# Queries and keys laid out by head pairs on GpSimd and transposed in 128x128 tiles

## The chip, the cores and the metric

The kernel runs on one core of one Trainium2 chip. The metric is device time in microseconds (us) for one execution. PE is TensorE, with PEld its weight loads, DVE is VectorE, ACT is ScalarE, POOL is GpSimd, SP is SyncE, which issues most DMAs. Each engine runs its own instructions in the order in which the program wrote them, and waits at semaphores for the others.

## The reference

Two layers follow each other: attention over chunks of 32 tokens with 8 memory slots per head, and a mixture of 8 experts with one expert a token.

```python
B, H, S, D = 4, 8, 768, 64                       # _attn_setup
for c in range(nc):                              # chunks of 32, 16 tokens left, 8 right
    k_full = np.concatenate([mem_k, k_ctx], axis=2)
    v_full = np.concatenate([mem_v, v_ctx], axis=2)
    scores = scale * np.matmul(q_c, k_full.transpose(0, 1, 3, 2))
    scores = scores - np.max(scores, axis=-1, keepdims=True)
    a = np.exp(scores)
    a = a / (np.sum(a, axis=-1, keepdims=True) + 1e-09)
    out[:, :, c_start:c_end] = np.matmul(a, v_full)
...
x = attn_out.transpose(0, 2, 1, 3).reshape(B * S, H * D)
logits = x @ w_gate                              # 8 experts, width 512 -> 1024 -> 512
disp[e, pos] = x[i]                              # in order of tokens, up to the capacity
h = np.maximum(np.einsum('ecd,edf->ecf', disp, w1), 0.0)
y = np.einsum('ecf,efd->ecd', h, w2)
out[i] = gate_w[i] * y[expert_idx[i], pos[i]]
```

## The kernel before

The attention stage works on 12 segments of 256 tokens (`segs`, 3 for each of 4 batches) and, within them, on 24 tiles of 128 tokens. One pass of `for t in range(NTL)` (L192) is one tile; even t begins segment t / 2. A segment's q and k come with one DMA each (`load_q`, `load_k`, 512 KB) into a ring of four slots in `raw2`: a partition holds two neighbouring tokens of one head side by side (`j` = 0, 1) and the 8 heads behind each other. They are loaded two segments ahead.

For the scores the head dimension has to stand on the partitions, with two heads (`hf` = 0, 1: an even and an odd head, a pair) on partitions 0 to 63 and 64 to 127. So q and k of segment n = t // 2 + 1 are transposed on PE one or two tiles ahead: `trans_k(n)` at even t, `trans_q(n)` at odd t, right behind the scores of the tile.

- `trans_q` (L453) makes 16 matmuls with the identity as the moving operand, each for one head and one `j`, 64 columns wide, into 64 partitions of a PSUM tile. The trace shows each as two passes. ACT copies two tiles of 128x512 into `qT` and interleaves the two tokens (L465).
- `trans_k` (L468) makes 8 transposes of 128x128 (L475), one for each head. The head's two tokens land on partitions 0 to 63 and 64 to 127, so ACT needs 8 copies of 64x256 (L480) into `KW`, one for each pair of `hf` and `j` and half of the heads. `KW` holds for each chunk of 32 tokens 24 keys of the chunks to the left, its own 32, and 8 memory keys. Then `copy_k` (L484) fills the 24: DVE does the odd heads, POOL the even ones from n = 2 on (L496, L498).

The rest of a tile: scores (L509, 16 matmuls), maximum and difference on DVE (L517, L520), exponent on ACT (L526), transposes of the weights of tile t - 1 (`trans_p`, L533), weights times values of tile t - 2 (`value`, L550) with the division on DVE (L553 to L558) and a column copy on POOL (L542), the transposes of the output (`trans_out`, L603) and the logits of earlier tiles. `VW` holds the values in two slots; `copy_v` (L414, L415) copies the overlaps on DVE, in part on ACT, and `load_v` brings the next 256 tokens in 8 DMAs. `route` decides each group's expert rows on DVE, and `put` (L803) writes rows of x to their slots with a DMA that POOL issues. From t = 14 to 21 POOL also subtracts for the split of the first expert's weights (L829), after ACT's cast (L828).

What sets the order is the program text alone: the block runs under `manual_schedule`, and each engine's queue is the order of the calls. POOL's queue is the one that the change touches most. Before the loop it fills `KW[1]` and `VW[1]` with zeros (L174, L136, L139) and the memory keys (L450); at t = 1 it makes the constants of the routing (L576 to L594); at t = 3 it copies the values of all memory slots (`memv`) into `ME` (L203), once their loads have landed. SP issues the loads of `memv` for the next batch at t = 0, 1 and 2 (L124), among those of k, q and v.

PSUM tiles come from a pool of 7 (`psum`). After the attention the experts run: `early` on the first 256 rows while routing ends, then `expert` for each of the 8.

Of the kernel before, what the change touches and what calls it, by code (L numbers as in the profile page):

```python
# [7 lines left out]
F32 = mybir.dt.float32  # L8
# [9 lines left out]
P = 128  # L18
B, H, S, DH, NMEM = 4, 8, 768, 64, 8
LEFT, CHUNK = 16, 32  # L20
# [30 lines left out]
class Kernel:  # L51
# [42 lines left out]
    def attention(self):  # L94
        tc, nc = self.tc, self.nc
# [5 lines left out]
        st = self.st  # L101
# [6 lines left out]
        memv = st.tile([64, 4, DH], F32, name="memv")  # L108
        self.ME = ME = st.tile([64, 2, 4, 65], F32, name="ME")
        self.preT = st.tile([P, 2, 8, B * H // 2], F32, name="preT")  # L110
        self.segs = segs = [(b, s) for b in range(B) for s in range(NSEG)]
        NS = len(segs)
        self.qn, self.kn, self.qT, self.pT, self.ex, self.xs = {}, {}, {}, {}, {}, {}
# [8 lines left out]
        def load_memv(b):  # L122
            for par in range(2):
                nc.sync.dma_start(out=memv[par * 32 + b * 8:par * 32 + b * 8 + 8],  # L124
                                  in_=self.mem_v[b].rearrange("(r u) m d -> u m r d", u=2)[par])
# [45 lines left out]
        for par in range(2):  # L171
            r = slice(par * 32, par * 32 + 8)
            nc.gpsimd.tensor_copy(out=ME[r, par, :, 0:64], in_=memv[r])
        nc.gpsimd.memset(KW[1][64:P, :, :, 0, :].rearrange("p a c d -> p (a c) d"), 0.0)  # L174
        self.fill_mem_v(0)
        self.load_k(2)
        self.load_q(2)
        zero_v(1, 0, None)
# [8 lines left out]
        def split1(t):  # L187
            if any(i == t for i, _ in PLAN):
                j = todo.pop(0)
                self.split(self.raw1, self.w1hi, self.w1lo, (slice(None), slice(None), slice(j, j + SPLIT1)), nc.gpsimd)  # L190

        for t in range(NTL):  # L192
            n = t // 2 + 1
            if t % 2 == 0 and n < NS:
                self.fill_mem_k(n)
            if t == 1:
                self.routing_setup()
            if t < 3:
                load_memv(t + 1)
            if t == 3:  # L200
                for par in range(2):
                    r = slice(par * 32, par * 32 + 32)
                    nc.gpsimd.tensor_copy(out=ME[r, par, :, 0:64], in_=memv[r])  # L203
            if t == 11:
                nc.sync.dma_start(out=self.raw1, in_=self.w1[0].rearrange("(k p) f -> p k f", p=P))
            self.scores(t)
            if n < NS:
                if t % 2 == 0:
                    self.trans_k(n)
                    if n + 2 < NS:  # L210
                        self.load_k(n + 2)
                else:
                    self.trans_q(n)
                    if n + 2 < NS:
                        self.load_q(n + 2)
            self.exps(t)
            if 0 <= t - 1 < NTL:
                self.trans_p(t - 1)
            if 0 <= t - 2 < NTL:
                self.value(t - 2)  # L220
            if 0 < t <= NTL - VB:
                self.copy_v(t - 1)
            k = (t - 2) // VB + 2
            if t > 1 and (t - 2) % VB == VB - 1 and k < B * NVB:
                self.fill_mem_v(k)
                self.load_v(k)
            if t == 22:

                nc.sync.dma_start(out=self.raw2, in_=self.w2[0].rearrange("(k p) d -> p k d", p=P))
            split1(t)  # L230
            self.tick(t > 20)
            if 0 <= t - 3 < NTL:
                self.trans_out(t - 3)
            if 0 <= t - 4 < NTL:
                self.logits(t - 4)
            for _ in range(3 if t > 20 else 1):
                self.tick(True)
            for _ in range(2 if t > 20 else 1):
                if self.puts:
                    self.put(*self.puts.pop(0)[:2])  # L240
            if t - 4 in ends:
                self.routes.append([self.route(ends[t - 4]), 1])
# [210 lines left out]
    def trans_q(self, n):  # L453
        nc = self.nc
        t = self.qT[n] = self.wk.tile([P, 4, SEG], F32, name="qT")
        src = self.qn.pop(n)
        for i in range(2):
            ps = self.psum().rearrange("p (r j t) -> p r j t", r=2, j=2)

            for r in range(2):  # L460
                for j in range(2):
                    for hf in range(2):
                        nc.tensor.matmul(ps[hf * 64:hf * 64 + 64, r, j, :], src[:, 4 * i + 2 * r + hf, j * 64:j * 64 + 64],  # L463
                                         self.ident, start=True, stop=True)
            (nc.vector.tensor_copy if n == 0 and i else nc.scalar.copy)(  # L465
                out=t[:, 2 * i:2 * i + 2, :].rearrange("p r (t j) -> p r j t", j=2), in_=ps)

    def trans_k(self, n):  # L468
        nc = self.nc
        kw = self.KW[n % NKW]  # L470
        src = self.kn.pop(n)
        for i in range(2):
            ps = self.psum().rearrange("p (h t) -> p h t", h=4)
            for h in range(4):
                nc.tensor.transpose(out=ps[:, h, :], in_=src[:, 4 * i + h, :], identity=self.ident)  # L475
            ps = ps.rearrange("p h (m t) -> p h m t", t=16)
            for hf in range(2):
                r = slice(hf * 64, hf * 64 + 64)
                for j in range(2):
                    (nc.vector.tensor_copy if n == 0 and i else nc.scalar.copy)(out=kw[r, 2 * i:2 * i + 2, :, hf, 24 + j:56:2], in_=ps[j * 64:j * 64 + 64, hf::2])  # L480
        if n:
            self.copy_k(n)

# [533 lines left out]
```

## Time and profile before

| what | value |
|---|---|
| median of 3 runs | 511.56 us |
| the three runs | 510.7, 511.56, 1536.18 us |
| the profiled execution | 508.52 us |
| its span, first to last instruction | 506.7 us |
| mean granted TensorE clock | 0.977 |
| PE, PEld busy | 461.3 us (91%), 394.1 us (78%) |
| DVE, ACT, POOL busy | 295.4 us (58%), 233.8 us (46%), 115.4 us (23%) |

One of the three runs took three times as long as the others; the median leaves it out. The two others and the profiled execution lie within 3.1 us. The page's strip by 40 slices of 12.7 us shows two stages: in the first 11 or 12 slices DVE and ACT are about as busy as PE, after that PE alone is near full. A row of the timeline gives start and length in us, engine, line, operation and operands, and in brackets for how long the engine had been idle and what ended that. Several equal instructions in a row are merged (x8).

### The profile page before, as it was taken

To read this page: it belongs to the slowest core of one execution; us is meant where nothing else is said; L and a number is where in the kernel's file an instruction comes from. 1 tells how busy PE (TensorE), PEld (TensorE's weight loads), DVE (VectorE), ACT (ScalarE), POOL (GpSimd) and SP (SyncE) were. 2 spreads that over 40 slices of the span, in tenths; PEclk is the share of its full clock that TensorE was granted. 3 is DMA by queue.
4 is the path that set the end of the run, shared out by engine and by line. 5 is a ranking of instruction groups with operands and counts; after the bars stand their busy time and mean duration, and the time that the engine had idled before them with its cause. 6 is when DMAs were issued, how large, how long until landed. Compare 5 with 4: busy or idle time off the path is not lost.

```text
span 506.7 us, 11689 instructions
## 1 busy us (share of the span) xinstructions
PE 461.3 (91%) x4317; PEld 394.1 (78%) x4317; DVE 295.4 (58%) x678; ACT 233.8 (46%) x462; POOL 115.4 (23%) x151
## 2 busy tenths in 40 slices
PE   7889988998868599898999999999999999889993
PEld 6778776777558579787888899799988989767782
DVE  6899797999854723456555525726442565554410
ACT  6799778888432413325434314524330553433300
POOL 8531133554623370020100210010022011020011
PEclk9999999999997899999999999999999999989997
DMA  9697899974672585227472480543321644630010
GB/s 212 152 213 157 198 272 261 208 200 104 134 273 93 177 303 169 108 70 266 160 243 61 156 294 15 190 154 125 125 87 50 217 172 167 225 115 2 4 41 38
DMA packets 77816, 78.71 MB, mean 155 GB/s; under 512 B 31762, under 2 KB 58510, under 8 KB 77648
## 3 DMA queue, kind: packets, MB, share of 16 engines
q1 hardware_dynamic: 72848, 61.93, 42.6%
q0 software_dynamic: 4800, 14.95, 7.7%
q8 instruction: 55, 0.90, 0.8%
q14 instruction: 113, 0.93, 0.6%
HBM read 60.86 MB, written 15.99 MB: 152 GB/s over the span
## 4 chain that ended last, share of the span: by engine, by line
issue 37%; DMA 34%; PE 16%; DVE 7%; ACT 2%; SPq 2%; POOLq 1%; DVEq 0%; POOL 0%; ACTq 0%
DMA out_dram<-y,tok 27%; DMA x_d<-pad,pads 4%; PE ps L509 3%; PE ps L463 3%; PE ps L550 3%; PE ps L533 2%; ACT kw L480 2%; DVE vw L415 1%; PE ps L332 1%; PE ps L475 1%; PE ps L603 1%; DMA raw<-in_q_dram 1%; DMA vw<-in_v_dram 1%; SPq L397 1%; DMA xg<-x_d 1%
## 5 line engine op out<-in xcount | busy, mean ns | idle before, releaser
L912 PE MATMUL p<-w2hi,hhi 128*128 128x512 f32 x224 | 92.7, 414 | 6.5 <-ACT w2hi L854 5.1
L872 ACT ACTIVATE hhi<-p 128x384 fp32r<-128x384 f32 (+2 forms) x68 | 33.7, 497 | 140.2 <-PE p L863 118.1
L919 POOL DMA_INDIRECT out_dram<-y,tok x28 | 32.0, 1144 | 279.1 <-DVEq L847 142.3
L912 PE MATMUL p<-w2lo,hhi 128*128 128x512 f32 x224 | 89.1, 398 | 0.0
L912 PE MATMUL p<-w2hi,hlo 128*128 128x512 f32 x224 | 88.7, 396 | 0.0
L873 DVE SCALAR_TENSOR_TENSOR hlo<-p,hhi 128x384 fp32r<-128x384 f32 (+2 forms) x68 | 37.6, 564 | 70.6 <-ACT hhi L872 47.0
L863 PE MATMUL p<-xhi,w1hi 128*128 128x256 f32 (+5 forms) x288 | 57.6, 322 | 4.1 <-issue 2.5
L863 PE MATMUL p<-xlo,w1hi 128*128 128x256 f32 (+5 forms) x288 | 57.2, 321 | 0.0
L863 PE MATMUL p<-xhi,w1lo 128*128 128x256 f32 (+5 forms) x288 | 57.1, 321 | 0.0
L912 PEld LDWEIGHTS p<-w2hi,hhi 128*128 128x128 f32 x224 | 42.9, 191 | 15.0 <-ACT w2hi L854 5.3
L918 DVE TENSOR_SCALAR y<-p,xg 128x512 f32<-128x512 f32 x28 | 21.0, 749 | 56.7 <-PE p L912 33.9
L912 PEld LDWEIGHTS p<-w2hi,hlo 128*128 128x128 f32 x224 | 42.7, 191 | 10.1
L863 PEld LDWEIGHTS p<-xhi,w1hi 128*128 128x128 f32 x288 | 45.3, 189 | 6.7 <-issue 3.2
L912 PEld LDWEIGHTS p<-w2lo,hhi 128*128 128x128 f32 x224 | 42.9, 192 | 7.8
L863 PEld LDWEIGHTS p<-xlo,w1hi 128*128 128x128 f32 x288 | 46.2, 190 | 2.1
L863 PEld LDWEIGHTS p<-xhi,w1lo 128*128 128x128 f32 x288 | 46.0, 189 | 2.0
L843 ACT CAST xhi<-px 128x512 fp32r<-128x512 f32 x34 | 19.8, 587 | 49.4 <-PE px L839 28.2
L855 DVE TENSOR_TENSOR w2lo<-raw,w2hi 128x512 fp32r<-128x512 f32 x64 | 41.2, 687 | 0.7
L480 ACT COPY kw<-ps 64x256 f32<-64x256 f32 x92 | 35.7, 388 | 10.8 <-PE ps L475 9.6
L844 DVE TENSOR_TENSOR xlo<-px,xhi 128x512 fp32r<-128x512 f32 x34 | 23.4, 691 | 28.1 <-ACT xhi L843 23.7
L829 DVE TENSOR_TENSOR w1lo<-raw,w1hi 128x512 fp32r<-128x512 f32 x56 | 36.6, 686 | 2.5 <-ACT w1hi L828 1.3
L550 PE MATMUL ps<-vw,pT 128*32 128x130 f32 x768 | 29.4, 277 | 8.4 <-issue 4.7
(156 smaller groups left out, 712.9 us busy)
## 6 DMA issues: line engine op xcount, KB each, us to landing
raw<-in_moe_w_dram SPq DMA_DIRECT2D x16, 2048.0 KB
raw<-in_q_dram SPq DMA_DIRECT2D x11, 512.0 KB
raw<-in_k_dram SPq DMA_DIRECT2D x10, 512.0 KB
vw<-in_v_dram SPq DMA_DIRECT2D x57, 64.0 KB
xg<-x_d SPq DMA_DIRECT2D x3, 792.0 KB
vw<-in_v_dram SPq DMA_DIRECT2D x31, 72.0 KB
xg<-x_d SPq DMA_DIRECT2D x4, 528.0 KB
xg<-x_d SPq DMA_DIRECT2D x2, 1056.0 KB
```

Of the source, the lines that this page charges most:

```text
L480: (nc.vector.tensor_copy if n == 0 and i else nc.scalar.copy)(out=kw[r, 2 * i:2 * i + 2, :, hf, 24 + j:56:2], in_=ps[j * 64:j * 64 + 64, h ...
L550: nc.tensor.matmul(ps[32 * c4:32 * c4 + 32, i * 130:i * 130 + 130], pT[:, pr * P + 32 * c4:pr * P + 32 * c4 + 32], vw[:, c + c4 + 1, :, pr ...
L829: (eng or self.nc.vector).tensor_tensor(out=lo[sl], in0=raw[sl], in1=hi[sl].bitcast(F32), op=ALU.subtract)
L843: nc.scalar.copy(out=self.xhi[:, d:d + k, sl], in_=pv)
L844: nc.vector.tensor_tensor(out=self.xlo[:, d:d + k, sl], in0=pv, in1=self.xhi[:, d:d + k, sl].bitcast(F32), op=ALU.subtract)
L855: self.nc.vector.tensor_tensor(out=self.w2b[j // 4][:, j % 4], in0=self.raw2[:, j], in1=self.w2a[:, j].bitcast(F32), op=ALU.subtract)
L863: self.nc.tensor.matmul(ps, a[:, d, fs], b[:, d, o:o + w], start=(i + d == 0), stop=(i == 2 and d == KD - 1))
L872: self.nc.scalar.activation(out=self.hhi[hs], in_=ps, func=AF.Relu)
L873: self.nc.vector.scalar_tensor_tensor(out=self.hlo[hs], in0=ps, scalar=0.0, in1=self.hhi[hs].bitcast(F32), op0=ALU.max, op1=ALU.subtract)
L912: self.nc.tensor.matmul(ps, a[:, f, t * P:t * P + P], b, start=(f == 0 and i == 0), stop=(f == KF - 1 and i == 2))
L918: nc.vector.tensor_scalar(out=y, in0=ps, scalar1=self.xg[e % 2][:, t, D:D + 1], scalar2=None, op0=ALU.mult)
L919: nc.gpsimd.indirect_dma_start(out=self.out[:, :], out_offset=bass.IndirectOffsetOnAxis(ap=tok[:, t:t + 1], axis=0), in_=y, in_offset=None ...
```

## The change

A new function `side(t)` lets POOL copy a loaded segment into one of two new SBUF tiles, `sd[0]` for q and `sd[1]` for k, so that the two heads of a pair stand side by side in a row of 128 elements, with one `j` behind the other. It is two copies of 128x512 for each of q and k (22 sides, 44 copies). `side(0)` and `side(1)` stand before the loop, right behind the zeros of `KW[1]`; `side(t + 1)` stands at the start of pass t, ahead of the scores, from t = 1 on. Odd t lays out the keys and even t the queries that PE transposes one pass later.

`side_by_side` then makes 8 transposes of 128x128 for q as for k, which write every second column of PSUM, so the two tokens come out interleaved and the two heads on the two halves of the partitions. ACT copies q with two plain 128x512 copies, and k with four copies of 64x512. Segment 0 keeps the old way.

```diff
+        self.sd = [st.tile([P, 4, 2, 2 * DH], F32, name=f"side{i}") for i in range(2)]
...
         self.fill_mem_v(0)
+        self.side(0)
+        self.side(1)
         self.load_k(2)
...
+            if t:
+                self.side(t + 1)
             self.scores(t)
...
         for i in range(2):
+            if n:
+                ps = self.side_by_side(0, i)
+                nc.scalar.copy(out=t[:, 2 * i:2 * i + 2, :], in_=ps)
+                continue
...
+    def side(self, t):
+
+        n, i = t // 2 + 1, 1 - t % 2
+        if n < len(self.segs):
+            src = (self.qn, self.kn)[i][n].rearrange("p (r h) (j d) -> p r j h d", h=2, j=2)
+            for j in range(2):
+                self.nc.gpsimd.tensor_copy(out=self.sd[i][:, :, j].rearrange("p r (h d) -> p r h d", h=2), in_=src[:, :, j])
+
+    def side_by_side(self, k, i):
+        ps = self.psum().rearrange("p (r t) -> p r t", r=2)
+        for r in range(2):
+            for j in range(2):
+                self.nc.tensor.transpose(out=ps[:, r, j::2], in_=self.sd[k][:, 2 * i + r, j], identity=self.ident)
+        return ps
...
         for i in range(2):
+            if n:
+                ps = self.side_by_side(1, i).rearrange("p r (m t) -> p r m t", t=CHUNK)
+                for hf in range(2):
+                    r = slice(hf * 64, hf * 64 + 64)
+                    nc.scalar.copy(out=kw[r, 2 * i:2 * i + 2, :, hf, 24:56], in_=ps[r])
+                continue
```

In the orders below the line numbers of the changed kernel are a little higher (L136 is L137 there, L203 is L206, L450 is L455, L496 is L526, L542 is L572); L483 is the copy in `side`, L489 the transpose in `side_by_side`; `side_110` is `sd[1]` (keys), `side_109` is `sd[0]` (queries), `raw_69` the ring of loaded segments, `kw_102` and `kw_103` the two `KW`.

POOL before the loop, from the zeros of `KW[1]` to the memory keys, before:

```order
L174 MEMSET kw_103 64x32x64
L136 MEMSET vw_105 64x9x260
L139 MEMSET vw_105 64x9x4
L136 MEMSET vw_105 64x9x260
L139 MEMSET vw_105 64x9x4
L450 COPY kw_103<-preT 64x32x8
```

and now:

```order
L175 MEMSET kw_103 64x32x64
L483 COPY side_110<-raw_69 128x4x128 x2
L483 COPY side_109<-raw_69 128x4x128 x2
L137 MEMSET vw_105 64x9x260
L140 MEMSET vw_105 64x9x4
L137 MEMSET vw_105 64x9x260
L140 MEMSET vw_105 64x9x4
L455 COPY kw_103<-preT 64x32x8
```

Four copies have come in between the zeros of `KW[1]` and those of `VW[1]`.

POOL from the end of the routing's constants (t = 1) to the key copy of t = 4, before:

```order
L594 MEMSET ones 128x128
L496 COPY kw_102<-kw_102 64x4x7x24
L542 COPY xr<-tok 128x1
L203 COPY ME<-memv 32x4x64 x2
L542 COPY xr<-tok 128x1
L450 COPY kw_103<-preT 64x32x8
L496 COPY kw_103<-kw_103 64x4x7x24
```

and now:

```order
L624 MEMSET ones 128x128
L483 COPY side_110<-raw_69 128x4x128 x2
L483 COPY side_109<-raw_69 128x4x128 x2
L526 COPY kw_102<-kw_102 64x4x7x24
L572 COPY xr<-tok 128x1
L206 COPY ME<-memv 32x4x64 x2
L483 COPY side_110<-raw_69 128x4x128 x2
L572 COPY xr<-tok 128x1
L455 COPY kw_103<-preT 64x32x8
L483 COPY side_109<-raw_69 128x4x128 x2
L526 COPY kw_103<-kw_103 64x4x7x24
```

The keys of segment 2 are laid out behind the routing's constants, and those of segment 3 behind the copies of `memv`.

PE at t = 2 and 3, from the scores of t = 2 on, before:

```order
L509 MATMUL ps<-kw_103,qT 32x128 x16
L475 MATMUL ps<-ident,raw_69 128x128 x8
L533 MATMUL ps<-ident,d 128x128 x4
L550 MATMUL ps<-vw_104,pT 32x130 x16
L509 MATMUL ps<-kw_103,qT 32x128 x16
L463 MATMUL ps<-ident,raw_69 64x128 x16
```

and now:

```order
L539 MATMUL ps<-kw_103,qT 32x128 x16
L489 MATMUL ps<-ident,side_110 128x128 x8
L563 MATMUL ps<-ident,d 128x128 x4
L580 MATMUL ps<-vw_104,pT 32x130 x16
L539 MATMUL ps<-kw_103,qT 32x128 x16
L489 MATMUL ps<-ident,side_109 128x128 x8
```

The transposes keep their places in PE's queue; they read what POOL wrote in place of what the DMA wrote, and the 16 matmuls for q have become 8.

More of the change, by code (lines that the diff above doesn't have):

```diff
@@ L464, in trans_q @@
                                          self.ident, start=True, stop=True)
-            (nc.vector.tensor_copy if n == 0 and i else nc.scalar.copy)(
+            (nc.vector.tensor_copy if i else nc.scalar.copy)(
                 out=t[:, 2 * i:2 * i + 2, :].rearrange("p r (t j) -> p r j t", j=2), in_=ps)
+    def side(self, t):
[10 more added lines that the diff above has]
+        return ps
     def trans_k(self, n):
@@ L479, in trans_k @@
                 for j in range(2):
-                    (nc.vector.tensor_copy if n == 0 and i else nc.scalar.copy)(out=kw[r, 2 * i:2 * i + 2, :, hf, 24 + j:56:2], in_=ps[j * 64:j * 64 + 64, hf::2])
+                    (nc.vector.tensor_copy if i else nc.scalar.copy)(out=kw[r, 2 * i:2 * i + 2, :, hf, 24 + j:56:2], in_=ps[j * 64:j * 64 + 64, hf::2])
         if n:
```

## The prediction

> **What bounds the kernel now.** I read the windows first. The change lies in the attention stage, which fills the first 145 us or so. The columns are the window, its length, then busy us and instructions of PE, PEld, DVE, ACT and POOL, the granted clock, the DMA share and GB/s.
>
> ```profile
> 24.00:120.00 96.00, 87.94 (x1760) 72.07 (x1753) 84.69 (x242) 80.31 (x161) 33.29 (x57) 1.00 0.84 206
> 36.00:48.00 12.00, 12.00 (x232) 9.80 (x232) 11.25 (x31) 10.88 (x21) 1.87 (x5) 1.00 0.85 168
> 96.00:108.00 12.00, 10.69 (x197) 8.62 (x196) 11.29 (x32) 10.75 (x24) 7.65 (x11) 1.00 1.02 275
> ```
>
> PE, DVE and ACT are all 84 to 92% busy, so the sums alone do not say which one limits. What DVE waited for between 20 and 145 us (total, times, longest) decides it:
>
> ```profile
> DVE kw L496 <- ACT kw L480: 4.7, 4, 2.0
> DVE vw L415 <- DMA vw<-in_v_dram: 2.4, 3, 2.1
> DVE rc L553 <- PE ps L533: 2.1, 1, 2.1
> DVE ps L515 <- PE ps L550: 1.4, 1, 1.4
> DVE rc L553 <- PE ps L550: 0.9, 3, 0.5
> ```
>
> In 125 us DVE waits 11.5 us. Of this 3.5 us (L533, L515) lie behind 137 us, after the last segment's transposes, and 2.4 us are for the loads of v. Everything else is DVE work, back to back. So a faster PE or ACT can give the stage only what DVE still waits for from them: 4.7 + 0.9 = 5.6 us.
>
> **The change part by part.** PE and ACT first (start, us, engine, line, operation; then two groups of the page with mean ns):
>
> ```profile
> 67.06 1.97 PE L463 MATMUL ps<-ident,raw 128*64 128x128 f32 x32
> 73.40 1.09 PE L475 MATMUL ps<-ident,raw 128*128 128x128 f32 x8
> L480 ACT COPY kw<-ps 64x256 f32<-64x256 f32 x92 | 35.7, 388 | 10.8 <-PE ps L475 9.6
> L465 ACT COPY qT<-ps 128x512 f32<-128x512 f32 x23 | 14.4, 692 | 1.6 <-PE ps L533 0.9 <-PE ps L463 0.6
> L535 ACT COPY pT<-ps 128x512 f32<-128x512 f32 x24 | 13.9, 577 | 0.2
> ```
>
> A segment's 32 passes for q take 1.97 us. Eight transposes, as k has them, take 1.09, so PE saves 0.88 us a segment, 9.7 us over the 11 changed ones. ACT's eight copies of a segment's keys (8 x 388 = 3.10 us) become four of 64x512. Their nearest row is L535, 577 ns, so 2.31 us. The two query copies lose their interleaving: 692 to 577 ns each. Together ACT saves 1.02 us a segment, 11 us in all. The new transposes write PSUM with a gap of one column. No row shows that, so it costs between 0 and a second pass (1.09 / 8 = 0.14 us each, 16 a segment, 24 us of PE); I take 0, nearest to L475, which writes as many columns.
>
> Because DVE limits, I book of those 20 us only what DVE waits for: between 0 and 5.6 us, and I take 3.7, since the L496 waits fall away with a kw copy that ends 0.8 us sooner on a PE that is ahead, but the small ones need not.
>
> POOL pays for it:
>
> ```profile
> L496 POOL COPY kw<-kw 64x672 f32<-64x672 f32 x10 | 7.4, 739 | 40.5 <-ACT kw L480 17.9 <-PE ps L642 9.0 <-DVE m L517 7.4
> L498 POOL COPY kw<-kw 64x96 f32<-64x96 f32 x6 | 1.9, 318 | 0.0
> ```
>
> Those two rows give 0.73 ns an element, so about 0.62 us for 512 elements (bounds 0.32 and 0.74): 22 sides of two copies are 44 x 0.62 = 27 us, in a queue that was busy 33.3 of 96 us. The queue runs in order, and this is where I expect the loss.
>
> *The iterations t = 3 and 4.* The side of the keys of segment 3 stands behind the copies of `memv` into `ME` on POOL, and those wait for a load:
>
> ```profile
> 30.87 1.10 PE L475 MATMUL ps<-ident,raw 128*128 128x128 f32 x8
> 32.80 0.83 POOL L203 COPY ME<-memv 32x256 f32<-32x256 f32 x2 [7.10 <-DMA memv<-in_mem_v_dram]
> 35.06 0.61 DVE L496 COPY kw<-kw 64x672 f32<-64x672 f32 x1
> 16.78 2.64 SPq L426 DMA_DIRECT2D vw<-ME  x2
> 19.06 0.25 POOL L594 MEMSET ones<- 128x128 bf16 x1
> 20.95 1.09 PE L475 MATMUL ps<-ident,raw 128*128 128x128 f32 x8
> ```
>
> PE transposed these keys at 30.87; now it needs a side that starts after 33.63 at the earliest and takes 1.24 us. It may be later still: the four side copies before the loop (2.5 us) push the memsets of VW[1], for which SP's L426 waited, and all later loads in SP's queue, `memv` among them, by 0 to 2.5 us; I take 1.5. So PE starts at 34.9 to 37.4, I take 36.4. Behind it on PE stand trans_p, value and the next scores. The first four transposes (0.55), the hand-over (0.1) and four copies (2.3) put DVE's L496 at 36.4 + 2.95 = 39.35 in place of 35.06. That is 3.8 us of idle DVE, net of the next term (bounds 2.3 and 4.8).
>
> *The first iterations.* At t = 1 the side of segment 2 waits for the routing constants (L594, ends 19.31, now 2.5 us later) and ends near 23.05, where PE transposed at 20.95. Its key copies then end at 26.0, not 25.57: 0.5 us for DVE (bounds 0 and 2.1).
>
> *The clock.* A PE that idles that long has a price in this trace:
>
> ```profile
> 153.33 1.94 PE L323 MATMUL ps<-ident,xg 128*128 128x128 f32 x8 [3.53 <-DMA xg<-x_d]
> 150.00:153.00 3.00, 0.00 (x0) 0.92 0.59 183
> 153.00:157.00 4.00, 3.67 (x20) 0.50 0.24 92
> 157.00:161.00 4.00, 4.00 (x29) 0.71 0.29 113
> ```
>
> After 3.53 us without work the granted clock was 0.50 (the figure before the DMA share), and eight transposes took 1.94 us where 1.09 is usual. The stall at t = 4 is 4 to 6.5 us long. A mean of 0.92 over 3 us and of 0.71 over 4 us put the half clock from about 152.5 to 159.3, 6.8 us, in which PE loses 3.4; I take 1.5 (bounds 0 and 3.4). [...]
>
> *DVE against POOL.* Some DVE instructions wait for POOL:
>
> ```profile
> 95.62 0.67 DVE L415 COPY vw<-vw 24x768 f32<-24x768 f32 x1
> 96.32 1.40 POOL L829 TENSOR_TENSOR w1lo<-raw,w1hi 128x512 fp32r<-128x512 f32 x1 [1.93 <-ACT w1hi L828]
> 96.76 1.50 DVE L415 COPY vw<-vw 24x768 f32<-24x768 f32 x1 [0.17 <-DMA vw<-in_v_dram]
> 71.98 0.63 POOL L450 COPY kw<-preT 64x256 f32<-64x256 f32 x1
> 72.08 0.69 DVE L414 COPY vw<-vw 24x256 f32<-24x256 f32 x1
> 60.91 0.28 DVE L414 COPY vw<-vw 24x256 f32<-24x256 f32 x1
> 103.63 1.29 POOL L829 TENSOR_TENSOR w1lo<-raw,w1hi 128x512 fp32r<-128x512 f32 x1 [2.64 <-ACT w1hi L828]
> 103.80 0.69 DVE L517 TENSOR_REDUCE m<-ps 128x8 f32<-128x512 f32 x1
> 54.33 0.74 POOL L496 COPY kw<-kw 64x672 f32<-64x672 f32 x1 [9.01 <-PE ps L642]
> 56.86 0.68 DVE L415 COPY vw<-vw 24x1024 f32<-24x1024 f32 x1
> ```
>
> A copy within SBUF grew by 0.83 beside L829 and by 0.41 beside a POOL copy. L517, which reads PSUM, kept its 0.69. So the side costs DVE between 0 and one whole POOL copy a pair: 22 x 0.62 = 13.6 us. Where will it fall? The key side follows POOL's L496: from its end at 55.07 to DVE's next copy at 56.86 there are 1.8 us, in which DVE reads PSUM, and 1.24 fit. The query side follows PE's transposes of the segment before, where DVE runs L517 and L520, both on PSUM, 0.69 us each. Most pairs should miss, so I take 0.16 us a pair, 3.5 us, near the lower end.
>
> *POOL's lateness later.* From t = 14 on, L829 and the row puts stand ahead of the sides:
>
> ```profile
> 105.08 1.02 POOL L803 DMA_INDIRECT x_d<-xr,r_dst  x1 [0.16 <-issue]
> 107.10 1.09 PE L475 MATMUL ps<-ident,raw 128*128 128x128 f32 x8
> ```
>
> The side of t = 17 can start at 106.10 and ends at 107.34, 0.2 us late. Six such places, with DVE the later one at each: 0.5 us (bounds 0 and 2). SP's loads of k and q now wait for POOL's side, an iteration sooner than for PE's transposes, so they are not later: 0. Instruction counts of DVE stay the same: 0. [...]
>
> The sum: 0.5 + 3.8 + 1.5 + 3.5 + 0.5 - 3.7 = +6.1 us, rounded down to +5.5 because the losses partly hide in each other. The profiled execution took 508.52 us (span 506.7), so 514.0; the median of the runs shown is 511.56, 3.04 above it, so I give 517 us. After the stage the experts run PE-bound, and nothing there is timed by anything but the stage's end, so the shift goes through whole.
>
> **The rivals.**
> 1. *The waits are made up.* If `memv` lands as before (side done at 34.9, stall 2.3), the clock holds and the sides miss DVE, the sum is 0.5 + 2.3 + 0.5 - 3.7, about 0: 511.5. For it: PE and ACT get 20 us of slack. Against it: between these two rows DVE never waited, so there was nothing to make it up in:
>
> ```profile
> 25.60 0.51 DVE L496 COPY kw<-kw 64x672 f32<-64x672 f32 x1 [1.39 <-ACT kw L480]
> 50.11 1.40 DVE L415 COPY vw<-vw 24x1024 f32<-24x1024 f32 x2 [0.19 <-DMA vw<-in_v_dram]
> ```
>
> 2. *DVE waits for POOL at every pair* (the slower side). Place: L414 and L415 of copy_v, L496 of copy_k. If a pair costs the 0.62 us of one copy, 13.6 in place of 3.5: 527. It decides, that is it passes +2%, from 0.37 us a pair. For it: L829 cost its neighbour 0.83 of 1.40 us. Against it: the placing above.
> 3. *DVE is not the bound.* If its order has slack I do not see, PE's 9.7 us count and only 0.5 + 3.8 stay against them: 506; with the t = 4 stall hidden, 502. Against it: the list of waits.
> [...]
>
> **How the numbers follow.** Forecast 0.55; rival 1 0.20; rival 2 0.13; rival 3 0.07; rival 4 0.05. Two percent of 511.56 is 10.2 us, about what a measurement of this kernel can tell from no change: faster means under 501.3, slower over 521.8. Faster: the lower edge of rival 3 and what I overlook, 0.03. Slower: most of rivals 2 and 4 (0.15) and the upper edge of the forecast (0.02): 0.17. The rest, 0.80, is within 2%. The range 507 to 524 takes in rival 1, the forecast with its bounds and the lower part of rival 2; it leaves out under 1 in 10 below and about 1 in 10 above. The forecast's own range is 513 to 521.
>
> **What would show it.** Right: PE idle at t = 4 for 4 us or more with POOL as releaser, DVE's L496 there near 39, the clock below 1.00 soon after, q's eight transposes at about 1.1 us, four key copies near 580 ns, side copies near 0.62 us, DVE busy 2 to 5 us more in 24 to 120 than before. Wrong: no PE wait for POOL at t = 4; DVE copies of vw as short as before; a stage that ends earlier than before by PE's saving; transposes longer than 1.1 us for eight.

## The result and the profile after

| | before | after |
|---|---|---|
| median | 510.75 us (17 runs) | 516.48 us (17 runs) |
| ratio, 95% interval | | 1.0085 [1.0057, 1.0113] |
| profiled execution, its span | 508.52, 506.7 us | 516.48, 514.7 us |
| PE, ACT busy | 461.3, 233.8 us | 456.5, 223.3 us |
| DVE, POOL busy | 295.4, 115.4 us | 308.6, 142.6 us |

The ratio is taken from the fast runs alone (14 of the 17 after the change), so it is not the quotient of the two medians. The change makes the kernel 0.85% slower by this ratio, 4.3 us, and 5.7 us slower by the medians. ACT lost 10.5 us of work and POOL gained 27.2 us, as the prediction has them (11 and 27). PE lost 4.8 us of the 9.7 forecast: the granted clock is lower here (0.970 in place of 0.977, more of it below), and in the run no_loop_sides, at 0.977, PE is busy 451.8 us, 9.5 less than before. But DVE, which executes the same 678 instructions, is busy 13.2 us longer.

The windows of the changed kernel (window, length, busy us and instructions of PE, PEld, DVE, ACT, POOL, then clock, DMA share, GB/s):

```profile
24.00:120.00 96.00, 76.86 (x1408) 61.73 (x1404) 88.62 (x217) 67.68 (x119) 50.78 (x87) 0.96 0.75 196
36.00:48.00 12.00, 11.62 (x173) 9.40 (x173) 10.38 (x26) 8.95 (x15) 6.84 (x14) 0.86 0.64 148
96.00:108.00 12.00, 9.29 (x189) 7.36 (x188) 11.59 (x22) 7.23 (x15) 9.25 (x14) 1.00 0.77 200
```

PE and ACT have room now: 77 and 68 of 96 us. DVE alone is near full, and in the same 96 us it gets through 217 instructions where it got through 242. What DVE waits for confirms that it limits (20 to 150 us; total, times, longest):

```profile
DVE kw L526 <- ACT kw L501: 2.9, 3, 1.4
DVE ps L545 <- PE ps L580: 1.4, 1, 1.4
DVE vw L420 <- DMA vw<-in_v_dram: 0.8, 1, 0.8
DVE rc L583 <- PE ps L633: 0.3, 1, 0.3
```

That is 5.4 us. The rows quoted in the prediction, up to 145 us, sum to 11.5, and up to 150 us there are 0.7 more. So DVE waited 6.8 us less, and lost 13.2 us by being slower itself. The 6.8 us are not all owed to a faster PE and ACT: in the run sides_unused below, where both have all their old work, DVE's waits in the same stretch are 8.7 us, so about half of the fall comes along with a slower DVE. The page's groups of the new operations (busy us, mean ns of one, then idle time ahead):

```profile
L483 POOL COPY side<-raw 128x512 f32<-128x512 f32 x44 | 28.2, 670 | 1.2 <-POOL xr L572 0.4 <-POOL kw L455 0.3 <-issue 0.2
L489 PE MATMUL ps<-ident,side 128*128 128x128 f32 x176 | 26.3, 293 | 4.5 <-POOL side L483 2.0 <-DVE kw L522 1.4 <-ACT pT L565 1.1
L501 ACT COPY kw<-ps 64x512 f32<-64x512 f32 x44 | 25.6, 581 | 11.4 <-PE ps L489 10.7
L465 ACT COPY qT<-ps 128x512 f32<-128x512 f32 x22 | 11.9, 594 | 0.2 <-PE ps L489 0.2
```

The operations cost about what was forecast. What they do to DVE is in a different place. DVE's copies within SBUF by shape, 24 to 150 us, before:

```profile
L415 DVE COPY vw<-vw 24x1024 f32<-24x1024 f32 x17 | 12.6, 743 | 2.5 <-DMA vw<-in_v_dram 2.3
L414 DVE COPY vw<-vw 24x256 f32<-24x256 f32 x14 | 5.1, 366 | 0.2
L450 DVE COPY kw<-preT 64x256 f32<-64x256 f32 x6 | 2.9, 481 | 0.2
L498 DVE COPY kw<-kw 64x96 f32<-64x96 f32 x6 | 1.3, 212 | 0.0
```

and the same lines after:

```profile
L420 DVE COPY vw<-vw 24x1024 f32<-24x1024 f32 x19 | 15.7, 825 | 1.2 <-DMA vw<-in_v_dram 0.8
L419 DVE COPY vw<-vw 24x256 f32<-24x256 f32 x14 | 9.6, 689 | 0.2
L455 DVE COPY kw<-preT 64x256 f32<-64x256 f32 x6 | 5.0, 836 | 0.1
L528 DVE COPY kw<-kw 64x96 f32<-64x96 f32 x6 | 2.4, 408 | 0.0
```

The same copies of the same size take up to twice as long (the window takes in two more of the first group after the change). Instructions that read PSUM did not change: the maximum (L517, now L547) takes 685 ns on average before and after, the difference (L520, now L550) 689. The timelines separate this further. Of the 79 copies within SBUF that DVE starts from 20 to 150 us after the change, the 35 that overlap no POOL instruction are together 0.2 us longer than the shortest of their shape in the kernel before. The 44 that overlap one are together 18.0 us longer. In the kernel before, the same sum over the 36 copies that overlap a POOL instruction is 6.4 us. The difference, 11.6 us, is most of the 13.2. One of the copies on the timeline, with the rows of DVE and of POOL (start, us, engine, line):

```profile
61.38 0.76 DVE L588 TENSOR_TENSOR xr<-ps,rc 128x256 f32<-128x256 f32 x2
62.15 2.19 DVE L420 COPY vw<-vw 24x1024 f32<-24x1024 f32 x1
...
59.71 0.74 POOL L526 COPY kw<-kw 64x672 f32<-64x672 f32 x1 [6.78 <-PE ps L580]
60.40 0.49 POOL L572 COPY xr<-tok 128x1 f32<-128x1 f32 x1
60.83 1.17 POOL L483 COPY side<-raw 128x512 f32<-128x512 f32 x2
61.95 0.18 POOL L572 COPY xr<-tok 128x1 f32<-128x1 f32 x1
62.07 0.61 POOL L455 COPY kw<-preT 64x256 f32<-64x256 f32 x1
62.62 1.17 POOL L483 COPY side<-raw 128x512 f32<-128x512 f32 x2
```

POOL's run of copies ends at 63.79, and DVE's copy ends 0.55 us after that, little less than it needs alone (the prediction's row of the same shape: 0.68). That fits a copy that stood still for 1.5 us, through three copies of POOL, not one. L588 ahead of it, which reads PSUM beside a side, kept its usual length (0.76 us for two, as L558 before). And the two sides stand in one run because POOL's queue had been held up for 6.78 us ahead of L526, so that the side of one tile slid up against that of the next.

### The profile page after: what moved, and what is told of

It reads as the page before. It is cut to its first block, busy times and chain, and to the rows that moved or that the text cites. A ratio compares the mean times of both kernels' runs of the same rounds, so it can differ in the third digit from the quotient of the medians.

```text
span 514.7 us, 11187 instructions
## 1 busy us (share of the span) xinstructions
PE 456.5 (89%) x4053; PEld 388.1 (75%) x4053; DVE 308.6 (60%) x678; ACT 223.3 (43%) x418; POOL 142.6 (28%) x195
## 4 chain that ended last, share of the span: by engine, by line
DMA 37%; issue 35%; DVE 13%; PE 6%; POOL 3%; SPq 2%; ACT 2%; POOLq 1%; another core or an unknown queue 0%; DVEq 0%; ACTq 0%
DMA out_dram<-y,tok 27%; DMA x_d<-pad,pads 4%; DVE vw L420 3%; DMA vw<-ME 3%; PE ps L580 2%; DMA memv<-in_mem_v_dram 2%; DVE xr L588 2%; DVE vw L419 1%; DVE m L547 1%; DVE d L550 1%; DMA vw<-in_v_dram 1%; ACT kw L501 1%; POOL vw L137 1%; PE ps L539 1%; PE ps L633 1%
## 5 line engine op out<-in xcount | busy, mean ns | idle before, releaser
L893 PE MATMUL p<-xhi,w1hi 128*128 128x256 f32 (+5 forms) x288 | 58.7, 326 | 3.0 <-DVE y L948 1.7
L580 PE MATMUL ps<-vw,pT 128*32 128x130 f32 x768 | 31.2, 287 | 15.8 <-issue 4.1
L874 DVE TENSOR_TENSOR xlo<-px,xhi 128x512 fp32r<-128x512 f32 x34 | 23.3, 691 | 27.8 <-ACT xhi L873 27.2
L580 PEld LDWEIGHTS ps<-vw,pT 128*32 128x32 f32 x768 | 22.2, 113 | 23.2 <-issue 6.3
```

What stands on the lines that cost most here:

```text
L580: nc.tensor.matmul(ps[32 * c4:32 * c4 + 32, i * 130:i * 130 + 130], pT[:, pr * P + 32 * c4:pr * P + 32 * c4 + 32], vw[:, c + c4 + 1, :, pr ...
L874: nc.vector.tensor_tensor(out=self.xlo[:, d:d + k, sl], in0=pv, in1=self.xhi[:, d:d + k, sl].bitcast(F32), op=ALU.subtract)
L893: self.nc.tensor.matmul(ps, a[:, d, fs], b[:, d, o:o + w], start=(i + d == 0), stop=(i == 2 and d == KD - 1))
```

## The experiments

All ratios are to runs of the kernel before on the same chip in the same job. The kernel before itself took 511.9, 513.0 and 505.0 us in the three jobs, so ratios are compared within a job. The changed kernel was in none of the three, so a comparison with its 1.0085 goes from one job to another. The busy times are those of one profiled execution each; those of q_only and apart took 4.5 and 5.6 us more than the medians of their runs.

| kernel | job | median us | ratio, 95% interval | DVE busy | POOL busy |
|---|---|---|---|---|---|
| no_loop_sides | 1 | 509.00 | 0.9962 [0.9928, 0.9996] | 297.2 | 118.4 |
| sides_unused | 1 | 523.79 | 1.0269 [1.0202, 1.0336] | 309.3 | 142.9 |
| side_before_me | 1 | 515.30 | 1.0064 [1.0023, 1.0105] | 305.2 | 141.6 |
| dma_layout | 1 | 516.62 | 1.0113 [1.0056, 1.0169] | 297.4 | 116.5 |
| q_only | 2 | 511.77 | 0.9947 [0.9900, 0.9994] | 300.5 | 129.6 |
| k_only | 2 | 515.54 | 1.0060 [1.0022, 1.0098] | 301.6 | 128.6 |
| half_sides | 2 | 511.16 | 0.9986 [0.9948, 1.0024] | 300.8 | 133.8 |
| act_sides | 2 | 511.71 | 0.9958 [0.9915, 1.0001] | 297.3 | 118.4 |
| seg1_old | 3 | 520.62 | 1.0296 [1.0241, 1.0352] | 302.2 | 139.6 |
| apart | 3 | 510.40 | 1.0091 [1.0053, 1.0128] | 302.8 | 142.0 |
| act_seg1_old | 3 | 511.70 | 1.0122 [1.0076, 1.0168] | 294.5 | 117.3 |
| q_act_seg1_old | 3 | 512.75 | 1.0142 [1.0092, 1.0193] | 294.4 | 117.0 |

### Job 1: take the side copies away, or add only them

*no_loop_sides*, the changed kernel without the 40 copies in the loop, so that PE transposes what segment 1 left in the two tiles:

```diff
-            if t:
-                self.side(t + 1)
```

> The changed kernel without the 40 side copies inside the loop; the four ahead of it stay. From segment 2 on PE transposes what segment 1 left in the two tiles, so the output is not the reference's; everything else runs as in the changed kernel. Theory A (the loss is mostly DVE waiting for the SBUF access while POOL's copies run): DVE's busy time falls from 308.6 us by 8 to 10, and the time falls under the kernel before: 502 to 507 us, ratio 0.985 to 0.993. Theory B (the loss is the order of POOL's queue: keys late at t = 2 and t = 4): the waits of PE for POOL go, 2 to 4 us in all, time about 512 to 514, ratio 1.003 to 1.006, DVE's busy time within 3 us of 308.6. Theory C (half clock after the stalls): as B, with the clock at 1.00 up to 145 us.

DVE's busy time fell to 297.2 us, 1.8 above the kernel before. That is theory A's sign. The time gained less than A expected: 0.4% under the kernel before, where A had 0.7 to 1.5%. DVE now waits longer for something else, the loads of v: 4.1 us, after 0.8 in the changed kernel and 2.4 in the kernel before.

*sides_unused*, the kernel before with the same 44 copies on POOL, read by nobody:

```diff
+            if t:
+                self.side(t + 1)
...
-            if n:
+            if 0:
                 ps = self.side_by_side(1, i).rearrange("p r (m t) -> p r m t", t=CHUNK)
```

> The kernel before with all 44 side copies on POOL that nobody reads: transposes and ACT's copies as before, the output is the reference's. Theory A: DVE's busy time is 304 to 310 us as in the changed kernel (before 295.4) and, with no saving on PE and ACT against it, the time is 518 to 524, ratio 1.014 to 1.026. Theory B: PE never waits for POOL, only the four copies ahead of the loop count, 511.5 to 513.5, ratio 1.002 to 1.006. Theory C: as B.

The copies alone cost 2.7% by the ratio, 11.9 us by the medians, and DVE's busy time rose by 13.9 us to 309.3. Both lie at the upper edge of what theory A has. No instruction reads what they write, and busy time holds no waits at semaphores. What can still wait is a load into a ring slot that a side copy has to read first, and POOL's own work behind the copies. The granted clock also fell below 1 here, with the old transposes of q and k in place:

```profile
24.00:120.00 96.00, 82.22 (x1582) 67.32 (x1582) 84.67 (x212) 71.59 (x145) 47.63 (x80) 0.96 0.74 193
```

*side_before_me* puts the side of t = 3 ahead of the copies of `memv` on POOL:

```diff
+            if t:
+                self.side(t + 1)
             if t == 3:
                 for par in range(2):
                     r = slice(par * 32, par * 32 + 32)
                     nc.gpsimd.tensor_copy(out=ME[r, par, :, 0:64], in_=memv[r])
...
-            if t:
-                self.side(t + 1)
```

> The changed kernel with the side of t = 3 ahead of the two copies of memv into ME in POOL's queue, nothing else. Theory A: only the stall at t = 4 goes, 1.5 to 2 us: 514 to 515.5, ratio 1.004 to 1.006. Theory B: 3 to 4 us go: 511.5 to 513.5, ratio 1.001 to 1.004. Theory C: the half clock from 36 to 40 us goes too and takes 1 us more with it.

In its profile DVE's maximum of tile 5 comes 5.66 us later than in the kernel before, and so does that of tile 4; in the changed kernel it is 3.55 us at tile 4 and 5.56 at tile 5. So the stall added about 2 us in the changed kernel, and it is gone here, but this run was already as late by tile 4 as the changed kernel is by tile 5, and nothing is gained. The ratio, 1.0064, lies inside the interval of the changed kernel, measured in another job: a gain can't be told from nothing.

*dma_layout* has no side copies on POOL; the loads of segments 1 to 11 (keys to 10) bring the layout, in two DMAs of 256 KB each with runs of 256 bytes:

```diff
+        dst = t.rearrange("p (j r) (h d) -> p j (r h) d", j=2, h=2)
+        for j in range(2):
+            self.nc.sync.dma_start(out=dst[:, j], in_=dap(src, o + j * DH, [[2 * DH, P], [HS, H], [1, DH]]))
```

> No side copies on POOL: the loads of q and k of segments 1 to 11 (keys to 10) bring the two heads side by side, with two DMAs of 256 KB in runs of 256 bytes in place of one of 512 KB in runs of 512. The last segment's keys go the old way. The output is the reference's. Theory A: DVE's busy time is back at 293 to 297 us, the savings of PE and ACT count for what DVE waited for, 503 to 508, ratio 0.985 to 0.995. Rival: shorter runs cost the DMA engines, the share of 0.84 (24 to 120 us) goes to 0.95 or more, v's loads come late, DVE waits for them 5 us more and the time is 511 to 516.

DVE's busy time is 297.4 us as without side copies, but what DVE waits for (20 to 150 us) has a new head:

```profile
DVE vw L420 <- DMA vw<-in_v_dram: 14.0, 5, 8.1
```

These waits were 2.4 us before, so the loads of v came late, by more than the rival's 5 us. The rival's reason is not shown: it asked for a DMA share of 0.95 from 24 to 120 us, and the share is 0.86 after 0.84. In SP's queue, in which the loads of v stand behind those of q and k, the new loads of q and k wait 9.6 us for PE (L561). Which of the two made v late was not separated.

### Job 2: halves, and another engine

*act_sides*: the 40 copies of the loop go to ACT.

```diff
-                self.nc.gpsimd.tensor_copy(out=self.sd[i][:, :, j].rearrange("p r (h d) -> p r h d", h=2), in_=src[:, :, j])
+                (self.nc.scalar.copy if t > 1 else self.nc.gpsimd.tensor_copy)(out=self.sd[i][:, :, j].rearrange("p r (h d) -> p r h d", h=2), in_=src[:, :, j])
```

> The 40 side copies in the loop go to ScalarE, at the same places of the program; nothing else changes. ScalarE has 223 us of work and gets about 40 x 0.58 = 23 us more, in the loop about 86 of 96 us. Theory A (the price is VectorE waiting while GpSimd copies): VectorE's busy time is back near 297 us and the time goes below the changed kernel's, 511 to 514 (ratio 1.000 to 1.004), if ScalarE does not become late. Rival D (the price is the copies' traffic in SBUF, whoever makes them): VectorE stays at 305 or more and the time at 516 or above. Rival E (ScalarE becomes the bound): VectorE's busy time falls, yet VectorE and TensorE wait longer for ScalarE than the 2.9 us now, and the time is 517 or more.

This is the run that tells most. Copies, data, tiles and places in the program are the same; only the engine differs. DVE's copies are back near their old length (24 to 150 us):

```profile
L420 DVE COPY vw<-vw 24x1024 f32<-24x1024 f32 x19 | 14.2, 748 | 4.5 <-DMA vw<-in_v_dram 4.1
L419 DVE COPY vw<-vw 24x256 f32<-24x256 f32 x14 | 5.6, 396 | 0.2
L455 DVE COPY kw<-preT 64x256 f32<-64x256 f32 x6 | 3.1, 511 | 0.2
L528 DVE COPY kw<-kw 64x96 f32<-64x96 f32 x6 | 1.4, 235 | 0.0
```

and the copy that took 2.19 us above takes 0.68. Others run beside ACT's side copies and keep 0.29 and 0.68 us:

```profile
60.20 0.68 DVE L420 COPY vw<-vw 24x1024 f32<-24x1024 f32 x1
...
76.34 0.29 DVE L419 COPY vw<-vw 24x256 f32<-24x256 f32 x1
76.55 0.68 DVE L420 COPY vw<-vw 24x768 f32<-24x768 f32 x1
...
75.76 1.14 ACT L483 COPY side<-raw 128x512 f32<-128x512 f32 x2
```

Rival D, the traffic in SBUF, falls. So does E in the main: DVE waits 4.9 us for ACT's key copies, 2.0 more than in the changed kernel, and 4.1 us for the loads of v, but the time is not 517. The ratio came out below the 1.000 to 1.004 of theory A and touches 1.

*q_only* and *k_only* lay out and transpose only the queries or only the keys the new way:

```diff
-        if n < len(self.segs):
+        if i == 0 and n < len(self.segs):
...
-            if n:
+            if 0:
                 ps = self.side_by_side(1, i).rearrange("p r (m t) -> p r m t", t=CHUNK)
```

> The queries the new way, with their 22 side copies; the keys as in the kernel before. So far: 44 side copies on the kernel before cost 2.7% (about 13.7 us), and the changed kernel is only 0.85% slower, so that the new transposes and copies out of PSUM give back about 9.4 us. Theory P (the gain is TensorE's, 8 full transposes a segment for 16 products of 64 columns, and it lies wholly in the queries): half the price and nearly all the gain, 511.9 + 6.9 - 9 = about 510, ratio 0.99 to 1.00. Theory S (the gain is ScalarE's fewer and larger key copies): half the price and little gain, about 517 to 518, ratio 1.010 to 1.013. If both count alike: 513 to 515.

> The keys the new way, with their 22 side copies; the queries as in the kernel before. TensorE saves nothing here (8 transposes a segment for 8), ScalarE's copies go from 8 to 4. Theory P: half the price of the side copies and no gain, about 518, ratio 1.010 to 1.014. Theory S: about 510, ratio 0.99 to 1.00. Both alike: 513 to 515. The two runs' differences to the kernel before should add up to that of the changed kernel, 4 to 5 us, if no part depends on the other.

The queries' half is slightly faster than the kernel before (0.5% by the ratio, 0.2% by the medians), the keys' half slower: nearer to theory P than to S, since what the change has to give lies mostly in the queries, where PE saves. But k_only is not as slow as P said, and the two do not add up. Their sum is +0.07%, where the changed kernel has +0.85%, with intervals of about 0.3 to 0.5 points to either side and another job. That remainder is left open.

*half_sides* moves half of the elements in each side copy from segment 2 on, and none of the rest:

```diff
-                self.nc.gpsimd.tensor_copy(out=self.sd[i][:, :, j].rearrange("p r (h d) -> p r h d", h=2), in_=src[:, :, j])
+                self.nc.gpsimd.tensor_copy(out=self.sd[i][:, 0:2 if t > 1 else 4, j].rearrange("p r (h d) -> p r h d", h=2), in_=src[:, 0:2 if t > 1 else 4, j])
```

> The side copies from segment 2 on move half of each segment's head pairs, so each has half the elements; the other half of the side tiles keeps segment 1's values. Number, order and waits of the copies are as in the changed kernel. Theory A (VectorE waits as long as GpSimd copies): without the 40 copies the kernel ran at 0.9962 of before, with them at 1.0085, so half the length gives the middle, about 1.002 (513 us), and VectorE's busy time falls from 308.6 by about 5 us. Rival B (the number of the copies and their place in GpSimd's queue matter, not their length): as the changed kernel, about 516, VectorE 307 or more.

Theory A held: 300.8 us of DVE and 0.9986, where rival B wanted 307 and 516 us. Length counts, and not the number of copies alone.

### Job 3: the start, the runs, and a combination

*apart* keeps number and length of the copies, but puts the second copy of each side elsewhere in POOL's queue:

```diff
-                self.side(t + 1)
+                self.side(t + 1, (0,))
...
                 self.trans_p(t - 1)
+            if t and t % 2 == 0:
+                self.side(t + 1, (1,))
...
+            if t % 2:
+                self.side(t + 1, (1,))
             split1(t)
```

> The two copies of a side stand apart in GpSimd's queue: the first where it was, the second after the probabilities' transposes (queries) or just ahead of the weight split (keys). Number and length of the copies are as in the changed kernel. Theory R (a copy of VectorE waits for GpSimd's whole run of copies, so long runs cost more than their sum; half the number and half the length each left only 4 to 6 of the 12 to 13 us): VectorE's busy time falls from 308.6 to 300 to 304, time 511 to 514 (ratio 0.999 to 1.005) if the later second copy keeps no transpose waiting. Rival T (only GpSimd's total copying time counts): VectorE at 307 or more, 515 to 517. Rival L (the second copies come late): VectorE falls, but TensorE's wait for GpSimd ahead of the transposes grows from 2.0 us to 4 or more, time as now.

On DVE's busy time theory R held. POOL is busy 142.0 us as in the changed kernel, DVE 302.8 in place of 308.6: the same copying, parted, holds DVE up less. That shorter runs are the reason is argued and not shown, since the second copies also stand beside other instructions now. On the time it missed: 1.0091. In the profiled execution DVE's waits grew from 5.4 to 9.2 us (20 to 150 us):

```profile
DVE vw L424 <- DMA vw<-in_v_dram: 5.4, 1, 5.4
DVE kw L530 <- ACT kw L505: 3.5, 3, 1.7
DVE rc L587 <- PE ps L584: 0.3, 1, 0.3
```

Rival L has a part in it: PE's wait for sides grew from 2.0 to 3.3 us, short of its 4.

*seg1_old* transposes segment 1 the old way, so that no side copies stand ahead of the loop:

```diff
-        self.side(0)
-        self.side(1)
...
-            if n:
+            if n > 1:
                 ps = self.side_by_side(0, i)
```

> Segment 1 goes the old way and has no side copies, so GpSimd's four copies ahead of the loop are gone; everything from segment 2 on is as in the changed kernel. Theory S1 (the two or three us by which the loop begins late stay to the end): ratio 1.001 to 1.004, 512 to 514, and VectorE's first maximum is no later than in the kernel before. Rival M (time lost at the start is made up later): as the changed kernel, 1.008, 516.

This missed by far, and in the other direction: 1.0296. Part of the reason is in its timeline. The copies of `memv`, forecast to hold up a side by 3.8 us in the changed kernel, did so here:

```profile
35.85 0.84 POOL L204 COPY ME<-memv 32x256 f32<-32x256 f32 x2 [7.53 <-DMA raw<-in_k_dram]
36.74 1.16 POOL L481 COPY side<-raw 128x512 f32<-128x512 f32 x2
37.41 2.31 PE L487 MATMUL ps<-ident,side 128*128 128x128 f32 x8 [4.31 <-POOL side L481]
```

They start 2.2 us later than in the changed kernel (33.63, below), PE waits 4.31 us for the side, and the clock drops (0.50 from 38 to 40 us): eight transposes take 2.31 us where 1.09 is usual. That is part of the 10.2 us that separate the medians of seg1_old and apart. How much of it is left at the end stays open: the experts' first transposes come at 164.4 us in its profile and at 163.6 in that of apart, an execution that at 516.0 us was itself 5.6 above its median.

*act_seg1_old* and *q_act_seg1_old* were meant as the best of both: segment 1 the old way, and the other side copies on ACT, for both or for the queries alone.

```diff
-                self.nc.gpsimd.tensor_copy(out=self.sd[i][:, :, j].rearrange("p r (h d) -> p r h d", h=2), in_=src[:, :, j])
+                self.nc.scalar.copy(out=self.sd[i][:, :, j].rearrange("p r (h d) -> p r h d", h=2), in_=src[:, :, j])
```

> All 40 side copies on ScalarE, and segment 1 the old way without any. If the two effects add (ScalarE's sides 0.9958, and 2 to 3 us from the start): ratio 0.988 to 0.993, 507 to 509, faster than both kernels. If the loop then waits for ScalarE or for the loads of v: 0.994 to 0.998.

> The same for the queries alone: 20 side copies on ScalarE, keys as in the kernel before. Theory P (the gain is TensorE's, in the queries; the keys' new way gives ScalarE 0.8 us a segment but costs it 1.2 in side copies here): as fast as or faster than the run with both, ratio 0.985 to 0.992. Theory S (ScalarE's larger key copies count): slower than the run with both, 0.995 or more.

Neither beats the kernel before in this job: 1.0122 and 1.0142, with DVE at 294.5 and 294.4 us of work. Against each other they are equal, so P and S are not told apart here. Within the job act_seg1_old and seg1_old differ in the copying engine alone, and the step from POOL to ACT is worth 520.62 - 511.70 = 8.9 us.

What stays open: why the kernel before is 1.6% faster on this third chip than on the second, and its variants are not. For this reason no version is claimed to beat the kernel before. q_only and act_sides are ahead by half a per cent in the second job, with intervals that end at 0.9994 and 1.0001, and the third job shows their relatives 1.2 and 1.4% behind.

## Why the prediction came out

The forecast was 517 us, +5.5; the median is 516.48, +5.7 to the 510.75 of the same runs. The place of the loss was right (POOL's copies, with DVE as the bound), but the sum came out by luck in part: its two terms of opposite sign for DVE and for PE and ACT were both too small. By its own steps:

- *DVE waiting for POOL, +3.5 (bounds 0 to 13.6).* This step failed. "Most pairs should miss, so I take 0.16 us a pair" is measured at 13.2 / 22 = 0.60 us a pair of DVE's busy time, the price of rival 2, and in the profile 16 of the 22 sides overlap a DVE copy that is over 0.05 us longer than the shortest of its shape before. The placing was misread where it was read from the trace. In the stretch from 55.07 to 56.86, in which DVE was said to read PSUM, the first half microsecond is a copy of its own within SBUF:

```profile
55.01 0.55 DVE L496 COPY kw<-kw 64x672 f32<-64x672 f32 x1 [1.98 <-ACT kw L480]
```

And the pairs did not stay where they were placed. POOL's L526 waits 20.1 us in all for ACT's key copies (L496 did so for 17.9), the sides behind it come in runs with other copies, and a DVE copy has lasted through up to three of them (the 2.19 us above). sides_unused, act_sides and half_sides show the cause: the copies, on POOL, by their length. How much of it is due to their coming in runs is not shown.
- *The gain of PE and ACT, -3.7 (0 to 5.6).* Without the price of the sides it is about 2 us, the 0.4% by which no_loop_sides and act_sides are ahead of before. Beside a DVE that is held up it seems to be more: in job 1 sides_unused and side_before_me, which differ in the new transposes with ACT's copies behind them and in one place of a side, lie 8.5 us apart, 4.1 us of it DVE's own busy time (309.3 and 305.2). Why was not tried. Something of this size has to be there, since rival 2's price did not make rival 2's time of 527, but its cause stays open.
- *The stall at t = 4, +3.8 (2.3 to 4.8).* The mechanism is right, its size was about 2 us. In the profile of the changed kernel:

```profile
33.63 0.97 POOL L206 COPY ME<-memv 32x256 f32<-32x256 f32 x2 [4.55 <-DMA memv<-in_mem_v_dram]
34.66 1.48 POOL L483 COPY side<-raw 128x512 f32<-128x512 f32 x2
35.44 0.33 PE L489 MATMUL ps<-ident,side 128*128 128x128 f32 x1 [1.57 <-POOL side L483]
39.41 1.42 DVE L526 COPY kw<-kw 64x672 f32<-64x672 f32 x1 [1.05 <-ACT kw L501]
```

DVE's L526 starts at 39.41; the forecast said 39.35. But PE waited 1.57 us and not 4, because the program as a whole was already about 3 us later: the maximum of tile 3 is 2.93 us late. A right time for one instruction is no proof of the sum that led to it.
- *The first iterations, +0.5 (0 to 2.1).* Measured 2.5 us at the first maximum and 2.9 to 3.8 in the next tiles. The cause isn't shown: the same maximum is 0.4 us late in q_only, and in sides_unused, which has the same four copies ahead of the loop, it is 2.4 us early and two tiles on 2.9 us late.
- *The clock, +1.5 (0 to 3.4).* The drop is there, as forecast: 0.86 from 36 to 48 us. It comes after less idle time than the row behind the forecast has, which is 3.53 us: PE paused for 1.57 us up to 35.44 and for 0.43 us up to 36.19, and the clock is 1.00 from 34 to 36 us and 0.60 in the next two.

```profile
36.00:38.00 2.00, 1.81 (x9) 1.81 (x10) 1.86 (x4) 1.00 (x2) 2.00 (x5) 0.60 0.68 138
```

But the term was too small, because other drops were not foreseen. The clock is also 0.50 from 24 to 26 us, behind a pause of PE of 3.86 us, and from 120 to 124, behind one of 3.00 us that ends at 118.91, 0.1 us after DVE's copy of 2.49 us shown in the last section. The mean of 0.96 over 24 to 120 us is 3.8 us of full clock, above the bound of 3.4; what that cost in time, with DVE as the bound, was not measured. no_loop_sides and sides_unused, in which no transpose waits for a side in the loop, have 0.96 there too.
- *POOL's lateness later, +0.5.* PE waits 2.0 us for sides in all, 1.57 of it at t = 4. The term holds.
- *Rival 3 (DVE not the bound)* falls by the list of waits and by DVE's 217 for 242 instructions. *Rival 4*, to which the prediction gives 0.05, stood for new transposes that cost more in themselves, by a slower clock or a PSUM write of twice the length. No run shows such a cost. Eight transposes into every second column take 1.09 us as before, and the clock dropped as much in sides_unused (0.96 from 24 to 120 us), which transposes as the kernel before does. That more transposes add to the drop is not excluded.

## What to carry to other kernels

Before work is moved to an idle GpSimd, look at which VectorE instructions run beside it. Here copies within SBUF that met a GpSimd copy took up to 2.2 us longer, instructions that read PSUM kept their 685 and 689 ns, and ScalarE made the same copies at no cost to VectorE's busy time (297.3 us, and 297.2 without them). Do not place such copies one by one in the trace of before: here a wait of 6.78 us at the head of GpSimd's queue moved two sides together, and the four VectorE copies that grew most, by 1.5 to 2.2 us, lay beside runs of three copies. Where several engines are near the limit, look for the next wait before a saving on one is booked: VectorE waited 2.4 us for the loads of v before the change, 4.1 us without the side copies in the loop and 14.0 us with the layout done by DMA.

## What the hardware showed that was not expected

A VectorE copy of 0.68 us took 2.19 us beside three GpSimd copies in a row. Another has the same pattern, with a scatter's issue and a run of three copies (DVE's row, then POOL's):

```profile
116.32 2.49 DVE L419 COPY vw<-vw 24x256 f32<-24x256 f32 x1
...
115.92 1.01 POOL L833 DMA_INDIRECT x_d<-xr,r_dst  x1 [0.16 <-issue]
116.94 0.61 POOL L455 COPY kw<-preT 64x256 f32<-64x256 f32 x1
117.49 1.16 POOL L483 COPY side<-raw 128x512 f32<-128x512 f32 x2
118.61 0.80 POOL L526 COPY kw<-kw 64x672 f32<-64x672 f32 x1
```

It ends at 118.81, 0.16 us after the sides, and such a copy takes 0.28 alone (the prediction's row of L414). In both cases POOL was at work when DVE's copy started, and DVE's copy is the one that grew. Where a DVE copy starts first, 0.05 us ahead of a side, it keeps its 0.68 us, and POOL's two copies take 1.67 us in place of 1.17. One engine standing still while the other copies would fit these rows; how that comes about is not shown.

```profile
86.52 0.68 DVE L420 COPY vw<-vw 24x1024 f32<-24x1024 f32 x1
86.57 1.67 POOL L483 COPY side<-raw 128x512 f32<-128x512 f32 x2 [0.15 <-issue]
```

The trace does not agree with itself on how much a DVE copy grows that starts while POOL is at work. In the first two cases it took 1.5 and 2.2 us more, beside three copies and the end of a scatter's issue, and ended only after the sides. In the next case it started 0.39 us after a side, took 0.58 us (0.51 is usual) and ended before the side did, and the side's two copies took 1.44 us in place of 1.17:

```profile
50.13 0.58 DVE L526 COPY kw<-kw 64x672 f32<-64x672 f32 x1
49.74 1.44 POOL L483 COPY side<-raw 128x512 f32<-128x512 f32 x2
```

What makes the difference between these places, the runs do not tell.
